# Shorter float64 decoding, sums of magnitudes on ScalarE in place of maxima on VectorE, and another order of the first tiles of the last layer's input product

## The chip, the core and the metric

The kernel runs on one core of one Trainium2 chip. The metric is the device time of one execution in microseconds (us). TensorE multiplies matrices into PSUM, VectorE (DVE in the rows) and ScalarE (ACT) work on tiles in SBUF and PSUM, GpSimd (POOL) on tiles in SBUF, and SyncE (SP) issues nearly all the DMAs. Each engine runs its own instructions strictly in the order of the program, and an instruction that waits holds back all that stand behind it on that engine.

## The reference

The inputs are an attention with mixed heads (batch 4, 12 heads, 448 positions, 64 channels) and two feed-forward blocks over 1792 = 4 x 448 tokens of 768 channels. The change touches only the blocks:

```python
def _moe_ref(x, w1, w2, w3, w_out):
    a = x @ w1
    b = x @ w2
    h = a * b @ w3
    return (h @ w_out).astype(np.float32)

def _moe2_ref(x, w_in, w_out):
    h = x @ w_in
    r = np.maximum(h, 0.0)
    g = r * r
    return (g @ w_out).astype(np.float32)
```

`w1`, `w2` are 768 x 1024, `w3` 1024 x 1024, `w_out` of the first block 1024 x 768, `w_in` of the second 768 x 2048 and its `w_out` 2048 x 768. All eight weight arrays of the two blocks arrive as float64, whose two 32-bit words the kernel turns into float32 itself.

## The kernel before, in words

**Stages.** After the attention (to about 425 us of the span) come the hidden products of the first block (`hidden_tile`, eight columns `fc` of 128 features, four groups of 448 tokens each), then M = w3 x w_out (`m_tile`, so that the two last products of the block become one), then the product of the hidden features with M (here "the x2 stage": four token groups `i`, six tiles `c` each), then the input product of the second block with ReLU and square (`layer_in`, `in_tile`), and the output product in halves of tokens (`multiply`).

**Precision.** Each operand of a product is split into a high and a low half, and three matmuls per pair of tiles add high x high, high x low and low x high. Before a split the tile is scaled by a power of two from the largest magnitude in it (`pow2`). Where the largest value over all 128 partitions is wanted, one number per partition is stored to DRAM and read back broadcast to all partitions: `crossing`, a DMA `across<-...` and then a DMA `ac<-across`, both issued on POOL; then VectorE takes the maximum (`acr<-ac`, line 863).

**Decoding.** `decode` takes a raw chunk of 128 x 768 doubles (`raw`, 768 KB, two buffers, loaded by SP at line 747): ScalarE takes the magnitude of the high word as float32 (`zt`, line 798), VectorE shifts the low word (line 799), clamps `zt` (line 803), joins the two (line 806); ScalarE takes the magnitude of the result in place and adds it up per partition (line 810), and VectorE puts the sign back from `raw` (line 812). `decode_alone` does the same for `w3` without ScalarE at the end. Decoded chunks of `w_in` and the last `w_out` go to DRAM (`kept_in`, `kept_out`) and come back when all chunks of their group of four (`IG`) are summed and the group's scale is known (`cast_in`: `ib<-kept_in` at line 1037, `w<-ib` at lines 1051 and 1052).

**What sets the order.** The program is written by a planner while it is built: `now` advances by fixed costs at every `tick`, `busy` holds a due time for ScalarE, VectorE and POOL, and streams of steps (weights, scales, halves) put their next instruction into the program as soon as the planner's time allows. DMAs of results are put off (`put_later`) and issued by `tick`. `need_in(j)` runs a stream by force when a weight is wanted that has not been written into the program yet.

**Around the first tiles of `layer_in`.** `layer_in((0, 1))` takes four columns `jj` of 128 features, with four token groups `i`: sixteen tiles of 18 matmuls. The scale factor of a tile (`sci`) is the product of the x2 scale `kx` and the weight scale. Twelve tiles (`i` from 0 to 2) come first, then `finish(x2_done[3])`, and the four tiles of `i = 3`, each behind its own `sci` (line 1649). The weights of column pair `q` may be fetched back only once `q <= pair_now[0] + 1`, and `pair_now` is set when `layer_in` of a pair begins. The four buffers of finished weights hold `jj` 0 to 3, and those of `jj` 4 and 5 take the buffers of `jj` 0 and 1.

Of the kernel before, what the change touches and what calls it, by code (L numbers as in the profile page):

```python
# [18 lines left out]
P = 128  # L19
CP = 112  # L20
F64_LEAST = 2.0 ** -15 * 1.125
F64_MOST = float.fromhex("0x1.dffffep+16")
# [13 lines left out]
def talking_heads_attention_moe_moe2(  # L36
# [696 lines left out]
    def load_w(i):  # L733
        kind, j = chunks[i]
        if kind == "wl":
            t = wo_tiles(j)[1]
# [23 lines left out]
    def decode_alone(raw, n):  # L760

        lo, hi = (raw.rearrange("p (f two) -> p f two", two=2)[:, :, w] for w in (0, 1))
        x = pools["w"].tile([P, DM], F32, tag="xa", name="xa", bufs=3)[:, :n]
        zt = pools["w"].tile([P, DM], F32, tag="zt", name="zt", bufs=1)[:, :n]
        xi, zi = x.bitcast(I32), zt.bitcast(I32)
        r = n / DM
        return x, [
            (ACT, 0.9 * r, lambda: nc.scalar.activation(zt, hi.bitcast(F32), AF.Abs)),
            (DVE, 0.55 * r, lambda: nc.vector.tensor_scalar(
                xi, lo, 29, 0x40000000, op0=ALU.logical_shift_right, op1=ALU.bitwise_or  # L770
            )),
            (DVE, 0.95 * r, lambda: nc.vector.scalar_tensor_tensor(
                xi, hi, -(2 ** 31), xi, op0=ALU.bitwise_and, op1=ALU.bitwise_or
            )),
            after(ACT),
            (DVE, 0.55 * r, lambda: nc.vector.tensor_scalar(
                zt, zt, F64_LEAST, F64_MOST, op0=ALU.max, op1=ALU.min
            )),
            (DVE, 0.55 * r, lambda: nc.vector.tensor_scalar(
                zi, zi, 4, 1, op0=ALU.logical_shift_left, op1=ALU.logical_shift_right  # L780
            )),
            (DVE, 0.95 * r, lambda: nc.vector.tensor_tensor(xi, zi, xi, op=ALU.bitwise_xor)),
            after(DVE),
        ]

    def decode(raw, n, total=None, x=None, zt=None):
# [10 lines left out]
        return x, [  # L797
            (ACT, 0.9 * r, lambda: nc.scalar.activation(zt, z, AF.Abs)),
            (DVE, 1.0 * r, lambda: nc.vector.tensor_scalar(
                xi, lo, 29, 0x40000000, op0=ALU.logical_shift_right, op1=ALU.bitwise_or  # L800
            )),
            (REST, HAND, None),
            (DVE, 0.6 * r, lambda: nc.vector.tensor_scalar(
                zt, zt, F64_LEAST, F64_MOST, op0=ALU.max, op1=ALU.min
            )),
            (DVE, 1.0 * r, lambda: nc.vector.scalar_tensor_tensor(  # L806
                xi, zt.bitcast(I32), 3, xi, op0=ALU.logical_shift_left, op1=ALU.bitwise_xor
            )),
            (REST, HAND, None),
            (ACT, 1.0 * r, lambda: nc.scalar.activation(x, x, AF.Abs, accum_out=total)),  # L810
            (REST, HAND, None),
            (DVE, 1.0 * r, lambda: nc.vector.scalar_tensor_tensor(
                xi, hi, -(2 ** 31), xi, op0=ALU.bitwise_and, op1=ALU.bitwise_or
            )),
        ]

# [155 lines left out]
    def one_steps(i):  # L972
# [26 lines left out]
        x, ops = (decode_alone if kind == "w3" else decode)(t, n)  # L999
        yield from read_raw(i, x, ops)  # L1000
        if kind == "w3":
            hh, ll = (
                pools["w"].tile([P, 4 * P], F32R, tag="wv"[z], name="w3", bufs=WB) for z in range(2)
            )
        elif j >= NFC // 2:
            yield POOL, 0, lambda: nc.sync.dma_start(kept[j], x)
            return
        else:
            hh, ll = wo_tiles(j)
# [169 lines left out]
    def largest(out, x):  # L1179
# [8 lines left out]
        (c0, c0 + 3, c0 + 4, c0 + 5, c1, c1 + 3, c1 + 4, c1 + 5),  # L1188
        (1, 1, 1, 1, 1, 1, 1, 1),
# [11 lines left out]
    def hidden_tile(ws, sc, hm, i, z, th, pt):  # L1201
        product(pt, [(two(ws[z][0]), cols_of(c), x) for c, x in enumerate(x_parts())], toks(i))
        if z == 0:
            nc.scalar.activation(th, pt[:, :S], AF.Copy, scale=sc[:, 0, i : i + 1])
            tick(1.13, 0.6)
        else:
# [3 lines left out]
            largest(hm[:, i : i + 1], th)  # L1210
            tick(1.13, 0, 1.2)
# [105 lines left out]

    def stage():
        return mlp.tile([P, S], F32, tag="st", name="st", bufs=16)
# [29 lines left out]
    hs = []  # L1349
    for fc in range(NFC):  # L1350
# [13 lines left out]
        for i in range(len(ths), B):  # L1364
            th = stage()
            for z in range(2):
                hidden_tile(ws, sc, hm, i, z, th, mm())
            ths.append(th)
        nc.vector.tensor_reduce(hm[:, B : B + 1], hm[:, :B], axis=AX.X, op=ALU.max)
        up, lo = pow2(hm[:, B : B + 1], 14, "hs")  # L1370
        nc.vector.tensor_copy(rows[:, 0, fc : fc + 1], lo)
        t = mp.tile([P, 2, NT], F16, tag="h", name="h", bufs=NFC)
        streams.append(Stream(halves_steps(
            [((t[:, 0, toks(i)], t[:, 1, toks(i)]), ths[i], up) for i in range(B)]
        )))
# [12 lines left out]
    def keep_m(f, acc, os_):  # L1388
# [132 lines left out]
    def x2_steps(i, ts, xm):  # L1521
# [5 lines left out]

        yield from crossing(xm[:, NDC:], 1, box, DVE)
# [6 lines left out]
    for i in range(B):  # L1535
# [3 lines left out]
        for c in range(NDC):  # L1539
# [4 lines left out]
            largest(xm[:, c : c + 1], pt[:, :S])  # L1544
            ts.append(t)
            if c < NDC - 1:
                tick(1.13, 0.6, 0.6)
        for o in range(2):
            a = slice(3 * o, 3 * o + 3)
            nc.vector.tensor_scalar(xm[:, a], xm[:, a], mlo[o], None, op0=ALU.mult)  # L1550
        nc.vector.tensor_reduce(xm[:, NDC:], xm[:, :NDC], axis=AX.X, op=ALU.max)
        x2_done.append(Stream(x2_steps(i, ts, xm)))
        streams.insert(0, x2_done[-1])
        tick(1.13, 0.6, 0.8)
# [78 lines left out]
    def layer_in(ps, gm):  # L1633
# [7 lines left out]
        n = B if ps[0] else B - 1  # L1641
# [305 lines left out]
```

## Time and profile before

| | |
|---|---|
| median of 3 runs | 1259.68 us (1258.32 to 1266.53) |
| the profiled execution | 1259.91 us, its span 1258.2 us |
| PE busy | 1233.0 us, 98% of the span |
| DVE, ACT, POOL busy | 926.9, 758.1, 527.1 us |
| granted TensorE clock, mean | 0.995 of full speed |

The profile counts an engine as busy while an instruction of it runs, and puts idle time down to what ended it. Line numbers (L1162) are those of the kernel before; names such as `mm<-x,w` read "tile written <- tiles read". In the columns of a stretch the granted clock is 1.00 at 2.4 GHz and 0.50 at 1.2 GHz.

### The profile page before, as it was taken

The page shows a single profiled execution, that of the slowest core. Times are in us where ns is not written, and L with a number is a line of the kernel's source. Part 1 is how long each engine was busy: PE and PEld are TensorE (multiplying, and loading weights), DVE is VectorE, ACT ScalarE, POOL GpSimd, SP SyncE. Part 2 cuts the span into 40 slices and gives each one's busy share as a digit, 9 for nine tenths or more (in the row PEclk, how much of TensorE's full clock was granted, in tenths as well). Part 3 has the DMA queues.
Part 4 walks back from the last instruction along what each step waited for, and adds up shares of the span by engine and source line. Part 5 has one row for each costly group of instructions (what it writes and reads, how often), then busy time and mean ns, then how long its engine had stood idle before and what let it go on. Part 6 is the DMA issues. An engine that isn't in the chain of part 4 may idle for free. (4 is left out here: it accounts for less than half of the span.)

```text
span 1258.2 us, 26105 instructions
## 1 busy us (share of the span) xinstructions
PE 1233.0 (98%) x10022; PEld 759.0 (60%) x10022; DVE 926.9 (74%) x1744; ACT 758.1 (60%) x1502; POOL 527.1 (42%) x537
## 2 busy tenths in 40 slices
PE   8999999999999999999999999999799999999998
PEld 4666666766776655555569955555355555665565
DVE  6888898798889858886849675765433664899673
ACT  6888888888888634543424353546664786665330
POOL 4897898889778401010003200000000414787340
PEclk9999999999999999999999999999899999999999
DMA  6456456555656734354313237567779876566562
GB/s 189 127 158 171 123 146 160 150 139 143 168 145 170 223 61 129 80 110 122 125 69 133 101 110 171 117 119 210 232 199 214 257 239 187 160 202 198 167 181 89
DMA packets 134562, 194.80 MB, mean 155 GB/s; under 512 B 33668, under 2 KB 111108, under 8 KB 134436
## 3 DMA queue, kind: packets, MB, share of 16 engines
q1 hardware_dynamic: 129972, 189.00, 53.9%
q0 software_dynamic: 1328, 1.72, 1.4%
q10 hardware_dynamic: 3136, 2.40, 0.7%
q8 instruction: 79, 1.29, 0.4%
q14 instruction: 47, 0.39, 0.1%
HBM read 109.88 MB, written 44.66 MB: 123 GB/s over the span
## 5 line engine op out<-in xcount | busy, mean ns | idle before, releaser
L1162 PE MATMUL mm<-x,w 128*128 128x448 f16 x2196 | 417.5, 353 | 8.2 <-ACT w L1051 8.1
L1162 PEld LDWEIGHTS <-w 128*128 128x128 f16 x2304 | 225.1, 98 | 219.5 <-ACT w L1051 8.5
L1779 PE MATMUL mm<-ow,ao 128*128 128x384 f16 x1176 | 191.7, 326 | 2.6 <-DVE st L1795 2.5
L285 PE MATMUL p<-Bt,wpre_k 120*120 120x448 f32 x360 | 159.3, 560 | 4.0 <-DMA Bt<-S 3.4
L1779 PEld LDWEIGHTS <-ao 128*128 128x128 f16 x1176 | 115.1, 98 | 79.2 <-issue 3.3
L381 PEld LDWEIGHTS <-EH 120*112 120x112 f16 (+1 forms) x1440 | 124.5, 130 | 44.0 <-issue 36.9
L403 DVE TENSOR_TENSOR ATl<-o,ATh 112x480 f16<-112x480 f32 x180 | 116.2, 645 | 24.2 <-ACT ATh L397 23.5
L354 POOL TENSOR_SCALAR EH<-E,st 120x448 f16<-120x448 f32 (+1 forms) x152 | 114.5, 761 | 44.3 <-DVE st L337 32.4
L307 ACT ACTIVATE E<-p,st 120x448 f32<-120x448 f32 x180 | 116.0, 644 | 21.4 <-DVE st L299 13.5
L397 ACT CAST ATh<-o 112x480 f16<-112x480 f32 x180 | 101.0, 561 | 42.6 <-PE o L381 37.8
L381 PE MATMUL o<-wph,EH 120*112 120x120 f16 x720 | 124.0, 219 | 0.8 <-DVE ATl L403 0.5
L381 PE MATMUL o<-wph,EL 120*112 120x120 f16 x720 | 122.0, 216 | 0.0
L381 PE MATMUL o<-wpl,EH 120*112 120x120 f16 x720 | 122.0, 216 | 0.0
L366 POOL TENSOR_TENSOR EL<-F,EH 120x448 f16<-120x448 f32 (+1 forms) x90 | 104.6, 1162 | 33.1 <-issue 20.1
L299 DVE TENSOR_REDUCE st<-p 120x1 f32<-120x448 f32 x180 | 110.2, 613 | 0.9 <-PE p L285 0.6
L1162 PE MATMUL mm<-h,M 128*128 128x448 f16 x576 | 109.8, 353 | 0.7 <-ACT M L1340 0.5
L810 ACT ACTIVATE xa<-xa 128x768 f32<-128x768 f32 x54 | 45.4, 841 | 88.6 <-DVE xa L806 80.1
L381 PEld LDWEIGHTS <-EL 120*112 120x112 f16 x720 | 93.6, 130 | 0.0
L368 DVE SCALAR_TENSOR_TENSOR EL<-E,st,EH 120x448 f16<-120x448 f32 (+1 forms) x90 | 82.7, 919 | 10.7 <-POOL EH L354 10.3
L1162 PEld LDWEIGHTS <-M 128*128 128x128 f16 x576 | 55.9, 98 | 53.9 <-DVE M L1336 2.1
L249 ACT COPY S<-s 110x896 f32<-110x896 f32 (+1 forms) x88 | 80.4, 913 | 9.7 <-PE s L242 8.9
L285 PEld LDWEIGHTS p<-Bt,wpre_k 120*120 120x120 f32 x360 | 57.1, 182 | 47.9 <-issue 17.9
(241 smaller groups left out, 2163.8 us busy)
## 6 DMA issues: line engine op xcount, KB each, us to landing
Bt<-S SPq DMA_DIRECT2D x176, 210.0 KB
raw<-in_moe_w_out_dram SPq DMA_DIRECT2D x24, 768.0 KB
g<-st SPq DMA_DIRECT2D x64, 224.0 KB
gt<-g SPq DMA_DIRECT2D x56, 256.0 KB
raw<-in_moe_w_in_dram SPq DMA_DIRECT2D x16, 768.0 KB
raw<-in_moe_w_dram SPq DMA_DIRECT2D x14, 768.0 KB
raw<-in_moe_w_dram SPq DMA_DIRECT2D x16, 512.0 KB
kept_in<-xa SPq DMA_DIRECT2D x16, 384.0 KB
```

The source lines that it names most:

```text
L249: nc.scalar.copy(Stile[s][:R, 2 * p : 2 * p + 2, :], Ps.pop((s, p))[:R, :, :S])
L285: nc.tensor.matmul(pt[: n * H, :S], wpre_k.rearrange("p t g -> p (t g)")[: n * H, : n * H], Bt.pop(u)[: n * H], start=True, stop=True,)
L299: nc.vector.tensor_reduce(nsum[u][:n, 0, j : j + 1], Pp[u][:n, :S], axis=AX.X, op=ALU.max, negate=True)
L307: nc.scalar.activation(e[:n], Pp.pop(u)[:n, :S].rearrange("p (a b) -> p a b", a=EG), AF.Exp, bias=t[:n, 0, j : j + 1], scale=1.0, accum_ou ...
L354: nc.gpsimd.tensor_scalar(seven(EH[u][:n]), Ex[u][:n], inverse(u), 1.0, op0=ALU.mult, op1=ALU.mult)
L366: nc.gpsimd.tensor_tensor(a, f, b, op=ALU.subtract)
L368: nc.vector.scalar_tensor_tensor(a, e, inverse(u), b, op0=ALU.mult, op1=ALU.subtract)
L381: nc.tensor.matmul(pt[:CP, c * n : (c + 1) * n], a[:n, c * CP : (c + 1) * CP], w[:n, :n], start=(i == 0), stop=(i == 2),)
L397: nc.scalar.copy(ATs[s][0][:, :, :, m * NR : m * NR + nr], src)
L403: nc.vector.tensor_tensor(ATs[s][1][:, :, :, a], src, ATs[s][0][:, :, :, a], op=ALU.subtract)
L1162: nc.tensor.matmul(pt[:, :S], w[a][:, cs], x[z][:, sl], start=(c == 0 and i == 0), stop=(c == len(parts) - 1 and i == 2),)
L1779: nc.tensor.matmul(pt[:, :OH], y[:, a, q * P : (q + 1) * P], ow[g, q][:, w, kb], start=(start and q == 0 and m == 0), stop=(q == NQ - 1 an ...
```

## The change

Six things change. (1) `decode` scales the high word by 2^-112 in the ScalarE pass, and the clamp on VectorE goes; the sign is joined before the last step, so that `raw` is read for the last time one VectorE step earlier and ahead of ScalarE's sum, which now writes into `zt` and is left out where no sum is wanted; `decode_alone` goes, and `w3` uses `decode`. (2) The maxima over the hidden tiles (except the first three token groups of column 0), over the x2 tiles and over M (except its last row tile) become sums of magnitudes on ScalarE (`magnitudes`), written to a tile `junk` that nobody reads. (3) The scale of a hidden column becomes a stream (`h_steps`). (4) The maximum over the six columns of an x2 group moves from the main program into its stream (`x2_steps`). (5) Stores to `kept` are put off. (6) In the first `layer_in` ten tiles come first, then six: (0,3), (1,3), (2,2), (2,3), (3,2), (3,3), and `pair_now` becomes 1 after the second of them.

```diff
-F64_LEAST = 2.0 ** -15 * 1.125
-F64_MOST = float.fromhex("0x1.dffffep+16")
+F64_BIAS = 2.0 ** -112
...
         if kind == "wl":
+            flush("kept")
...
-    def decode_alone(raw, n):
...
-            (ACT, 0.9 * r, lambda: nc.scalar.activation(zt, z, AF.Abs)),
-            (DVE, 1.0 * r, lambda: nc.vector.tensor_scalar(
-                xi, lo, 29, 0x40000000, op0=ALU.logical_shift_right, op1=ALU.bitwise_or
+            (ACT, 0.9 * r, lambda: nc.scalar.activation(zt, z, AF.Abs, scale=F64_BIAS)),
+            (DVE, 0.6 * r, lambda: nc.vector.tensor_scalar(
+                xi, lo, 29, 0, op0=ALU.logical_shift_right, op1=ALU.bitwise_or
             )),
-            (REST, HAND, None),
-            (DVE, 0.6 * r, lambda: nc.vector.tensor_scalar(
-                zt, zt, F64_LEAST, F64_MOST, op0=ALU.max, op1=ALU.min
+            (DVE, 1.0 * r, lambda: nc.vector.scalar_tensor_tensor(
+                xi, hi, -(2 ** 31), xi, op0=ALU.bitwise_and, op1=ALU.bitwise_or
             )),
+            (REST, 0.3, None),
             (DVE, 1.0 * r, lambda: nc.vector.scalar_tensor_tensor(
                 xi, zt.bitcast(I32), 3, xi, op0=ALU.logical_shift_left, op1=ALU.bitwise_xor
             )),
-            (REST, HAND, None),
-            (ACT, 1.0 * r, lambda: nc.scalar.activation(x, x, AF.Abs, accum_out=total)),
-            (REST, HAND, None),
-            (DVE, 1.0 * r, lambda: nc.vector.scalar_tensor_tensor(
-                xi, hi, -(2 ** 31), xi, op0=ALU.bitwise_and, op1=ALU.bitwise_or
-            )),
         ]
+        if total is not None:
+            ops += [
+                after(DVE),
+                (ACT, 1.0 * r, lambda: nc.scalar.activation(zt, x, AF.Abs, accum_out=total)),
+            ]
...
+                magnitudes(*n_mags.pop())
+                tick(1.13, 1.4)
...
+                n_mags.append((hm[:, i : i + 1], th))
+                tick(1.13, 0, 0.65)
...
+    def magnitudes(out, x):
+        nc.scalar.activation(junk[:, : x.shape[-1]], x, AF.Abs, accum_out=out)
...
+    def h_steps(fc, hm, t, ths):
...
+        for a in last:
+            yield ACT, 0.8, lambda: magnitudes(*a)
+        yield after(ACT)
+        yield DVE, 1.4, scale
...
-                yield DVE, 0.45, lambda: largest(mx[:, f, o : o + 1], M32[f][o])
+                yield ACT, 0.75, lambda: magnitudes(mx[:, f, o : o + 1], M32[f][o])
...
+        yield after(ACT)
+        yield DVE, 0.3, lambda: nc.vector.tensor_reduce(
+            xm[:, NDC:], xm[:, :NDC], axis=AX.X, op=ALU.max
+        )
         yield from crossing(xm[:, NDC:], 1, box, DVE)
...
-            largest(xm[:, c : c + 1], pt[:, :S])
+            magnitudes(xm[:, c : c + 1], t)
...
-        n = B if ps[0] else B - 1
+        late = [] if ps[0] else [(jj, B - 1) for jj in (0, 1)] + [
+            (jj, i) for jj in (2, 3) for i in (B - 2, B - 1)
+        ]
+        early = [(jj, i) for jj in sc for i in range(B) if (jj, i) not in late]
+        n = B - 1 if late else B
...
-        for jj, i in [(jj, i) for jj in sc for i in range(n)]:
+        for jj, i in early:
             in_tile(gm, jj, i, *sc[jj])
-        if n < B:
+        if late:
             finish(x2_done[n])
             for jj in sc:
                 nc.vector.tensor_scalar(sc[jj][1][:, n:], kx[:, n:], need_in(jj)[1], None, op0=ALU.mult)
-                in_tile(gm, jj, n, *sc[jj])
+        for jj, i in late:
+            in_tile(gm, jj, i, *sc[jj])
+            if (jj, i) == (1, B - 1):
+                pair_now[0] = 1
```

**SyncE, the fetch of the weights of `jj` 4 to 7.** `ib<-kept_in` are these fetches, `g<-st` stores of finished tiles, `raw` loads of chunks. Before:

```order
L1127 DMA g_12890<-st 128x448 x3
L1127 DMA kept_out_350<-xa 128x768
L1127 DMA g_12890<-st 128x448 x6
L1037 DMA ib<-kept_in_332 128x768
L1037 DMA ib<-kept_in_333 128x768
L1037 DMA ib<-kept_in_334 128x768
L1037 DMA ib<-kept_in_335 128x768
```

And now:

```order
L1102 DMA g_12805<-st 128x448
L1102 DMA kept_out_350<-xa 128x768
L1102 DMA g_12805<-st 128x448 x4
L1012 DMA ib<-kept_in_332 128x768
L1012 DMA ib<-kept_in_333 128x768
L1102 DMA g_12805<-st 128x448 x4
L1012 DMA ib<-kept_in_334 128x768
L1012 DMA ib<-kept_in_335 128x768
```

The fetch for `jj` 4 and 5 stood behind the stores of fifteen tiles of `layer_in`, and stands behind those of ten.

**VectorE, around the scale of x2 group 3 (`xs`, from line 863 on, in the change line 837).** `im` is the top of a group of four weight chunks, `xa<-...` are steps of a decoding. Before, after five decodings without the last step of the fifth:

```order
L806 SCALAR_TENSOR_TENSOR xa<-zt,xa 128x768
L1026 TENSOR_REDUCE im<-isum 128x1
L863 TENSOR_REDUCE acr<-ac 128x1
L109 TENSOR_SCALAR xs<-acr 128x1
L110 TENSOR_SCALAR xs<-xs 128x1
```

And now, after five whole decodings:

```order
L780 SCALAR_TENSOR_TENSOR xa<-zt,xa 128x768
L1001 TENSOR_REDUCE im<-isum 128x1
L773 TENSOR_SCALAR xa<-raw 128x768
L776 SCALAR_TENSOR_TENSOR xa<-raw,xa 128x768
L837 TENSOR_REDUCE acr<-ac 128x1
L108 TENSOR_SCALAR xs<-acr 128x1
```

Two steps of a sixth decoding, which read the sixth chunk, stand ahead of the scale.

**VectorE, around the tile scales of `i = 3` (`sci`, 128x1).** `is` is the scale of a group of weight chunks, here of the third group. Before:

```order
L863 TENSOR_REDUCE acr<-ac 128x1
L109 TENSOR_SCALAR is<-acr 128x1
L110 TENSOR_SCALAR is<-is 128x1
L113 TENSOR_SCALAR is<-is 128x1
L114 RECIPROCAL is<-is 128x1
L1649 TENSOR_SCALAR sci<-kx,is 128x1 x4
L1052 SCALAR_TENSOR_TENSOR w<-ib,is,w 128x768 x2
```

And now:

```order
L1656 TENSOR_SCALAR sci<-kx,is 128x1 x4
L837 TENSOR_REDUCE acr<-ac 128x1
L108 TENSOR_SCALAR is<-acr 128x1
L109 TENSOR_SCALAR is<-is 128x1
L112 TENSOR_SCALAR is<-is 128x1
L113 RECIPROCAL is<-is 128x1
L1027 SCALAR_TENSOR_TENSOR w<-ib,is,w 128x768 x2
```

The four `sci` stand ahead of the scale of the third weight group. TensorE's rows are the same ones in the same sequence, but for the tiles that `layer_in` takes in another order.

## Rows read from the trace of the kernel before

**Rows 1.** The page: busy us, share of the span and instructions of each engine.

```profile
PE 1233.0 (98%) x10022; PEld 759.0 (60%) x10022; DVE 926.9 (74%) x1744; ACT 758.1 (60%) x1502; POOL 527.1 (42%) x537
```

**Rows 2.** Waits of PE: tile and line, what ended it, us in total, times, longest.

```profile
PE mm L1779 <- DVE st L1795: 2.5, 2, 1.8
...
PE mm L1409 <- POOL w L1013: 0.7, 2, 0.5
...
PE mm L1409 <- ACT w L1010: 0.4, 1, 0.4
```

**Rows 3.** Timeline around the gap: start, us, engine, line, instruction, [idle before <- releaser].

```profile
854.83 20.40 PE L1162 MATMUL mm<-x,w 128*128 128x448 f16 x107
...
882.82 6.46 SPq L1127 DMA_DIRECT2D g<-st  x6
...
885.00 0.29 DVE L863 TENSOR_REDUCE acr<-ac 128x1 f32<-128x128 f32 x1 [6.82 <-DMA ac<-across]
...
886.26 0.63 ACT L1656 ACTIVATE st<-mm,sci 128x448 f32<-128x448 f32 x1 [2.95 <-DVE sci L1649]
...
889.33 2.34 SPq L1037 DMA_DIRECT2D ib<-kept_in  x4
...
894.04 1.96 ACT L1051 ACTIVATE w<-ib,is 128x768 f16<-128x768 f32 x2 [2.79 <-DMA ib<-kept_in]
...
895.03 17.23 PE L1162 MATMUL mm<-x,w 128*128 128x448 f16 x81 [8.07 <-ACT w L1051]
```

**Rows 4.** Stretches of PE: from:to, length, busy us (instructions), granted clock, DMA share, GB/s.

```profile
892.00:893.00 1.00, 0.00 (x0) 0.50 1.21 344
...
898.00:899.00 1.00, 1.00 (x6) 0.87 0.00 0
```

**Rows 5.** Timeline of the first tiles of `layer_in` and of the decodings beside them.

```profile
828.09 0.92 ACT L798 ACTIVATE zt<-raw 128x768 f32<-128x768 f32 x1 [6.74 <-DMA raw<-in_moe_w_out_dram]
...
832.32 48.02 PE L1162 MATMUL mm<-x,w 128*128 128x448 f16 x253
...
839.09 1.13 ACT L1543 ACTIVATE st<-mm,ms 128x448 f32<-128x448 f32 x2
...
842.04 0.55 DVE L799 TENSOR_SCALAR xa<-raw 128x768 int32<-128x768 int32 x1
...
846.04 0.33 SPq L747 DMA_DIRECT2D raw<-in_moe_w_in_dram  x1
...
851.15 0.54 POOL L848 DMA_DIRECT2D ac<-across  x1 [7.97 <-DMA across<-xm]
855.43 0.92 ACT L798 ACTIVATE zt<-raw 128x768 f32<-128x768 f32 x1 [6.51 <-DMA raw<-in_moe_w_in_dram]
...
859.93 0.33 SPq L747 DMA_DIRECT2D raw<-in_moe_w_out_dram  x1
...
865.48 0.93 ACT L798 ACTIVATE zt<-raw 128x768 f32<-128x768 f32 x1 [2.68 <-DMA raw<-in_moe_w_out_dram]
...
867.98 0.28 DVE L863 TENSOR_REDUCE acr<-ac 128x1 f32<-128x128 f32 x1
...
869.05 3.46 ACT L1340 ACTIVATE x<-st,xs 128x448 f16<-128x448 f32 x6
```

**Rows 6.** Groups of instructions by shape: count, busy us, mean ns, idle before and its releasers.

```profile
L812 DVE SCALAR_TENSOR_TENSOR xa<-raw,xa 128x768 int32<-128x768 int32 x54 | 52.4, 970 | 31.6 <-ACT xa L810 31.6
...
L803 DVE TENSOR_SCALAR zt<-zt 128x768 f32<-128x768 f32 x55 | 31.3, 569 | 14.2 <-ACT zt L798 14.2
...
L1180 DVE TENSOR_REDUCE hm<-st 128x1 f32<-128x448 f32 x29 | 18.0, 620 | 1.0
```

**Rows 7.** The same view: ScalarE's square of a tile and the read of its sum.

```profile
L1657 ACT ACTIVATE st<-st 128x448 f32<-128x448 f32 x64 | 36.9, 577 | 2.0
...
L1657 ACT ACTIVATION_READ_ACCUMULATOR st<-st 128x1 f32 x64 | 11.9, 186 | 0.0
```

**Rows 8.** Stretch 722 to 832 us, the x2 stage: PE, PEld, DVE, ACT, POOL busy, clock, DMA.

```profile
722.00:832.00 110.00, 109.53 (x578) 56.26 (x579) 71.37 (x141) 49.97 (x88) 6.20 (x10) 1.00 0.59 135
```

More of the change, by code (lines that the diff above doesn't have):

```diff
@@ L998, in one_steps @@
             return
-        x, ops = (decode_alone if kind == "w3" else decode)(t, n)
+        x, ops = decode(t, n)
         yield from read_raw(i, x, ops)
+        yield after(DVE)
         if kind == "w3":
@@ L1209, in hidden_tile @@
             )
-            largest(hm[:, i : i + 1], th)
-            tick(1.13, 0, 1.2)
+            if n_mags is None:
+                largest(hm[:, i : i + 1], th)
+                tick(1.13, 0, 1.2)
+            else:
+                n_mags.append((hm[:, i : i + 1], th))
+                tick(1.13, 0, 0.65)
     def first_tile(n):
@@ L1316, in mm @@
         return ps_m.tile([P, 512], F32, tag="mm", name="mm")
+    junk = mlp.tile([P, S], F32, tag="junk", name="junk", bufs=1)
+    def magnitudes(out, x):
+        nc.scalar.activation(junk[:, : x.shape[-1]], x, AF.Abs, accum_out=out)
     def stage():
@@ L1348, in talking_heads_attention_moe_moe2, with scale @@
     kx = sm.tile([P, B], F32, tag="kx", name="kx", bufs=1)
-    hs = []
+    hs, mags = [], []
+    def h_steps(fc, hm, t, ths):
+        box = {}
+        def scale():
+            nc.vector.tensor_reduce(hm[:, B : B + 1], hm[:, :B], axis=AX.X, op=ALU.max)
+            box["up"], lo = pow2(hm[:, B : B + 1], 14, "hs")
+            nc.vector.tensor_copy(rows[:, 0, fc : fc + 1], lo)
+        last = list(mags)
+        mags.clear()
+        yield after(DVE)
+        for a in last:
+            yield ACT, 0.8, lambda: magnitudes(*a)
+        yield after(ACT)
+        yield DVE, 1.4, scale
+        yield from halves_steps(
+            [((t[:, 0, toks(i)], t[:, 1, toks(i)]), ths[i], box["up"]) for i in range(B)]
+        )
     for fc in range(NFC):
@@ L1366, in talking_heads_attention_moe_moe2 @@
             for z in range(2):
-                hidden_tile(ws, sc, hm, i, z, th, mm())
+                hidden_tile(ws, sc, hm, i, z, th, mm(), mags)
             ths.append(th)
-        nc.vector.tensor_reduce(hm[:, B : B + 1], hm[:, :B], axis=AX.X, op=ALU.max)
-        up, lo = pow2(hm[:, B : B + 1], 14, "hs")
-        nc.vector.tensor_copy(rows[:, 0, fc : fc + 1], lo)
         t = mp.tile([P, 2, NT], F16, tag="h", name="h", bufs=NFC)
-        streams.append(Stream(halves_steps(
-            [((t[:, 0, toks(i)], t[:, 1, toks(i)]), ths[i], up) for i in range(B)]
-        )))
+        streams.append(Stream(h_steps(fc, hm, t, ths)))
         hs.append(two(t))
@@ L1543, in talking_heads_attention_moe_moe2 @@
             nc.scalar.activation(t, pt[:, :S], AF.Copy, scale=mlo[c // 3])
-            largest(xm[:, c : c + 1], pt[:, :S])
+            magnitudes(xm[:, c : c + 1], t)
             ts.append(t)
             if c < NDC - 1:
[L1547 to L1551, printed above, removed]
+                tick(1.13, 1.35)
         x2_done.append(Stream(x2_steps(i, ts, xm)))
         streams.insert(0, x2_done[-1])
-        tick(1.13, 0.6, 0.8)
+        tick(1.13, 1.35)
     mid.close()
```

39 lines of the change are left out of this document (10 added, 29 removed).

## The prediction, made before the kernel was run

> **What bounds the kernel now.** I read the busy times first: TensorE is busy for 1233.0 of 1258.2 us [rows 1]. About 25 us can be won at all, whatever the change does for the other engines; the question is which of TensorE's idle times it touches. The waits of TensorE and the timeline say where these are: one gap of 8.07 us [rows 3], 1.1 us on the weights `w3` and 1.8 us, the longest of two, in the output product [rows 2]. The rest lies at the start and in the attention, where almost nothing changes.
>
> The gap is read backwards [rows 3]. TensorE waits for weights `jj` = 4 that ScalarE splits at 894.04. ScalarE waits for their fetch, which SyncE issued at 889.33 although nothing but its place in the queue held it: it stands behind six stores of tiles, and they wait for ScalarE's tiles. ScalarE waits 2.95 us for a tile scale on VectorE, and VectorE stands idle 6.82 us for the `ac<-across` of a weight group that is wanted much later. So the gap comes from the order of instructions in three queues. After it TensorE runs at 0.50 of its clock until the stretch from 898 [rows 4]: 81 matmuls take 17.23 us, where at the rate of the 107 before the gap (20.40 us) they would take 15.44. That is 1.79 us, including the wait for the low half of the first weight.
>
> **The change part by part.**
>
> *Decoding.* VectorE loses a clamp, 0.57 us, from each of the 54 chunks (the 55 calls of the row hold one for a shared buffer) and 29 maxima of 0.62 us [rows 6], then 24 over x2 and 14 over M of similar length. It is not the bound, so this counts only where it feeds TensorE. The place is `w3`: per chunk two short steps less, so high and low halves come earlier than the 0.4 and 0.7 us by which TensorE waited [rows 2]. Bounds: nothing, and 1.1 us; I take 1.1, since the two steps are most of a microsecond and three waits share it. If this cover were missing, the old waits are what returns.
>
> *Sums on ScalarE.* 67 of them, 0.58 us and 0.19 us for the read of the sum by the nearest row, the square of the same shape [rows 7]: 51 us on ScalarE, against which eight sums of chunks go. It was busy for 758.1 us of the span [rows 1]. In the x2 stage, the densest of the stages concerned, it would go from 49.97 us of 110 to 68 [rows 8]. What hides them is TensorE's own work: it is busy for 109.53 of these 110 us. A maximum takes 0.62 us, a sum 0.76, so the move would cost 67 x 0.14 = 9 us on a chain, and costs nothing as long as the tiles wait in PSUM. The Trainium skill, in "ScalarE: Activation LUTs" (rules for kernel authors), says that maxima and other simple arithmetic belong on VectorE rather than on ScalarE. The single instruction agrees with it, 0.62 against 0.76 us; by that rule the sum would be 9 us worse, by the rows of the stage it is not.
>
> *Order of the first tiles.* A tile takes (886.96 - 832.32) / 16 = 3.415 us, with 886.96 the start of the gap, 895.03 - 8.07 [rows 3, 5]. The fetch for `jj` 4 now stands behind the stores of ten tiles and no longer fifteen, and the scales of the tiles stand ahead of the `ac<-across` that held VectorE. So the gap of 8.07 us and its 1.79 us of slow clock go, if the fetch is in time (below).
>
> *What is late next.* x2 group 3 is now wanted after ten tiles, at 832.32 + 34.15 = 866.47, and no longer after twelve, at 873.3. Before, its halves began at 869.05 [rows 5]: 4 us ahead of the old need, but 2.6 us behind the new one. Its scale was not waiting for its crossing: `acr` at 867.98 shows no idle time before it [rows 5]. It stood behind five decodings, each behind its raw chunk. Now two steps of a sixth stand there too. Against that, a raw buffer comes free earlier: before, the load for the third chunk went out at 846.04, 4.0 us after the first step of the first chunk at 842.04; now it can go out after two VectorE steps, 0.55 + 0.97 = 1.5 us. A load takes 9.4 us (846.04 to 855.43) or 5.55 (859.93 to 865.48) [rows 5]. With these: chunk 1 frees its buffer at 843.6, chunk 2 at 846.4 (behind the sum of chunk 1 and its own first pass on ScalarE); chunk 3 arrives at 853.0, chunk 4 at 855.8, and ScalarE takes chunk 4 up to 857.4 behind the sum of chunk 3. Chunk 6 then arrives between 863.0 and 866.8. Two steps (1.5), `acr` to the first half (869.05 - 867.98 = 1.07) and a high and a low half (1.2, from 3.46 us for six) put the first columns at 866.8 to 870.6. TensorE waits 0.3 to 4.1 us at tile (0,3); I take 2.2, the middle, since both load times occur in this stretch. Below it the bound is nothing.
>
> *The fetch.* ScalarE must finish ten tiles before the tenth store. From the scale of group 3, at 865.6 to 869.4, it has six halves (3.46), five tiles of 0.63 + 0.58 + 0.19 = 1.4 and one sum (1.0) to do: 877.0 to 880.9. A fetch takes 4.7 us (889.33 to 894.04) [rows 3], or 9.4 like a raw chunk: it lands between 881.7 and 890.3. Tile 17 starts at 886.96 and the new wait, 887.3 to 891.1, and its first high half needs 0.98 us on ScalarE ahead of that. So it is in time, or late by about 1 us with the longest fetch. I take 0.
>
> *The sum*: -8.07 - 1.79 - 1.1 + 2.2 = -8.8 us, against the profiled execution's 1259.91: 1251.1. This execution stands 0.23 above the median of the runs, 1259.68, so the forecast is **1251** (1250.9). Ends: without the new wait and with the 1.8 us of the output product gone as well, 1247; with 4.1 us of waiting, 1 us for the fetch and no gain at `w3`, 1256.
>
> **The rivals.**
>
> *No new wait at all* (0.25). If loads of chunks take 5.5 us or less in this stretch, because fewer of them collide with the stores, group 3 is ready in time, and the time is 1259.68 - 10.96 = 1249. For it speaks the one load of 5.55 us, against it the two of 9.4 [rows 5]. The Trainium skill, in "DMA: Bandwidth & Descriptors" (anatomy of one DMA), gives a copy about 2.0 us plus its bytes at 436 GB/s, an estimate of 3.8 us for 768 KB. By that rule the sixth chunk would come at 861 and this rival would be the result; the trace disagrees, with 9.4 us.
>
> *The gap moves* (0.13). The fetch still stands behind ten stores in SyncE's queue, and these behind ScalarE, which also waits for raw chunks (6.51 us at 855.43 [rows 5]). One more such wait among tiles 6 to 10 moves the fetch from 877.0 to 880.9 to 883.5 to 887.4 and its landing to 888 to 897: TensorE waits 1 to 6 us more and may fall to the half clock again (1.8). That gives 1253 to 1259, about 1256.
>
> *ScalarE falls behind, and the kernel is slower* (0.10). The place is the x2 stage: ScalarE alone empties the tiles, and waits for raw chunks in its queue (6.74 us at 828.09). Before, it took the last two x2 tiles at 839.09, ending 7.9 us after TensorE was done with them at 832.32 [rows 5]. If none of its waits takes up the added sums, 24 x 0.76 = 18 us, the last x2 sum comes at 858. The crossing then decides: `ac<-across` waited 7.97 us for its first leg [rows 5], the second let VectorE idle for 6.82 us [rows 3], with their issue about 16. With 2.3 us of scale and halves the first columns come at 876.5, 10 us late, and 1.8 us of slow clock follow: 1259.68 - 10.96 + 11.8 = 1260.5. From about 16 us of lateness on, this eats the whole gain; each further 3.4 us is a tile more. Against it: ScalarE stood idle for 60 of the 110 us [rows 8], so most of the sums fit there.
>
> *My forecast* has 0.52.
>
> **How the numbers follow.** The likeliest case gives 1251. The range is 1247.5 to 1257.5: down to the case without a new wait less about one microsecond for the smaller waits, up past the forecast's own end of 1256 into most of the case where the gap moves. Outside lie the slower case and the tails, under 0.2. A difference of under 1%, 12.6 us, is about what this measurement can't tell from none. All the idle time that the change can reach, 8.07 + 1.79 + 1.1 + 1.8 = 12.8 us, is no more than that: faster by over 1% gets 0.05. Slower by over 1%, above 1272, needs the last rival with three more tiles lost: 0.04. The rest, 0.91, is within 1%, nearly all of it on the faster side.
>
> **What would show it.** The gap of 8.07 us before the weights of `jj` 4 should be gone and the clock stay at 1.00 there; SyncE's `ib<-kept_in` should go out near 879, and the four `sci` stand ahead of an idle VectorE. A wait of TensorE of 0 to 4 us should appear about 34 us after the first tile of `layer_in`, released by the halves of x2 group 3. The waits on `w3` should shrink below 0.3 us. VectorE's busy time should fall by some 90 us and ScalarE's rise by 45, without any change of the time from either. The forecast is wrong if the wait at group 3 is above 5 us, if TensorE still waits for `ib`, or if waits appear among the hidden or x2 tiles, where there are none now.

## The result, and the profile after

The changed kernel takes **1248.26 us** (median of 6 runs, 1247.43 to 1249.23) beside 1261.05 us for the kernel before (6 runs, 1258.32 to 1266.53) on the same chip: a ratio of 0.9896, 95% interval 0.9875 to 0.9916. The profiled execution took 1248.55 us, its span is 1246.8 us. The time is that of the rival without a new wait, 1249, and lies in the range; the forecast of 1251 was one term too high.

The page gives the busy time of each engine, to be read against [rows 1]:

```profile
PE 1230.0 (99%) x10022; PEld 757.8 (61%) x10022; DVE 845.8 (68%) x1581; ACT 793.6 (64%) x1628; POOL 523.9 (42%) x537
```

VectorE lost 81 us and ScalarE gained 36, both less than the 90 and 45 expected. Of TensorE's waits (what for, us in total, times, longest), the two on `w3` [rows 2] are gone; the output product still waits:

```profile
PE mm L1789 <- DVE st L1805: 2.4, 2, 1.7
```

The groups by shape (count, busy us, mean ns, idle before) show what replaced the clamp, the last sign step and the maxima of [rows 6]:

```profile
L780 DVE SCALAR_TENSOR_TENSOR xa<-zt,xa 128x768 int32<-128x768 int32 x54 | 52.9, 979 | 37.5 <-ACT zt L772 34.2
L776 DVE SCALAR_TENSOR_TENSOR xa<-raw,xa 128x768 int32<-128x768 int32 x54 | 52.4, 971 | 1.9
...
L1304 ACT ACTIVATE junk<-st 128x448 f32<-128x448 f32 x53 | 30.4, 573 | 14.8 <-DVE st L1186 14.1
...
L1304 ACT ACTIVATION_READ_ACCUMULATOR junk<-st 128x1 f32 x67 | 12.7, 190 | 0.0
```

The sign step on VectorE costs the same 0.97 us as in [rows 6], but its idle time ahead of it fell from 31.6 to 1.9 us, since it no longer stands behind ScalarE. The idle time has not gone: it has moved to the last step (L780), which stands idle for 37.5 us, 34.2 of them for ScalarE's first pass. What is gained is that `raw` has been read by then. The two rows of a sum, 0.573 and 0.190 us, add up to the 0.76 us estimated from [rows 7], but they overlap in time: one sum starts at 825.29, its read at 825.78 and ScalarE's next instruction at 825.87. What a sum costs is read below, from the kernel with the maxima put back. In the x2 stage (722 to 831 us: PE, PEld, DVE, ACT, POOL busy, clock, DMA) TensorE stays covered, as in [rows 8]:

```profile
722.00:831.00 109.00, 108.90 (x577) 56.32 (x577) 58.31 (x116) 69.58 (x140) 5.46 (x10) 1.00 0.65 148
```

The timeline of the stretch that [rows 3] and [rows 5] show of before (start, us, engine, line, instruction, idle before):

```profile
831.27 73.94 PE L1137 MATMUL mm<-x,w 128*128 128x448 f16 x390
...
833.09 0.56 DVE L773 TENSOR_SCALAR xa<-raw 128x768 int32<-128x768 int32 x1
...
834.73 0.33 SPq L747 DMA_DIRECT2D raw<-in_moe_w_in_dram  x1
...
838.00 0.33 SPq L747 DMA_DIRECT2D raw<-in_moe_w_in_dram  x1
...
846.81 0.93 ACT L772 ACTIVATE zt<-raw 128x768 f32<-128x768 f32 x1 [6.37 <-DMA raw<-in_moe_w_in_dram]
...
858.97 0.93 ACT L772 ACTIVATE zt<-raw 128x768 f32<-128x768 f32 x1 [1.15 <-DMA raw<-in_moe_w_out_dram]
...
861.53 2.91 ACT L1328 ACTIVATE x<-st,xs 128x448 f16<-128x448 f32 x5 [1.63 <-DVE kx L1529]
...
866.85 0.57 DVE L1656 TENSOR_SCALAR sci<-kx,is 128x1 f32<-128x1 f32 x4
...
872.32 1.28 SPq L1012 DMA_DIRECT2D ib<-kept_in  x2
...
875.54 0.29 DVE L837 TENSOR_REDUCE acr<-ac 128x1 f32<-128x128 f32 x1 [8.12 <-DMA ac<-across]
...
880.38 1.74 ACT L1026 ACTIVATE w<-ib,is 128x768 f16<-128x768 f32 x2
```

The first row is the result: 390 matmuls in one piece, where before 107 were followed by 8.07 us of nothing. The fetch of the weights of `jj` 4 goes out at 872.32 and they are split from 880.38 on; their tile comes at 831.27 + 16 x 3.41 = 885.9. The 8.12 us that VectorE idles for the crossing of a weight group are still there, now behind the four `sci` and so with nobody waiting. The clock (stretch, busy, granted clock), which was 0.50 at 892 to 893 in [rows 4]:

```profile
890.00:895.00 5.00, 5.00 (x28) 1.00 0.93 295
```

### The profile page after: what moved, and what is told of

It reads as the page before. It is cut to its first block, busy times and chain, and to the rows that moved or that the text cites. A ratio compares the mean times of both kernels' runs of the same rounds, so it can differ in the third digit from the quotient of the medians.

```text
span 1246.8 us, 26161 instructions
## 1 busy us (share of the span) xinstructions
PE 1230.0 (99%) x10022; PEld 757.8 (61%) x10022; DVE 845.8 (68%) x1581; ACT 793.6 (64%) x1628; POOL 523.9 (42%) x537
## 4 chain that ended last, share of the span: by engine, by line
PE 89%; DVE 5%; DMA 3%; ACT 2%; issue 0%; SPq 0%; ACTq 0%; POOL 0%; DVEq 0%
PE mm L1137 42%; PE mm L1789 15%; PE p L284 9%; PE o L380 7%; PE mm L1412 5%; PE s L241 5%; PE a L494 4%; DMA Bt<-S 2%; PE p L1137 2%; DVE ATl L402 1%; DVE st L298 1%; DVE EL L367 1%; DMA x<-x_d 1%; ACT E L306 1%; DMA vraw<-in_v_dram 0%
## 5 line engine op out<-in xcount | busy, mean ns | idle before, releaser
L380 PEld LDWEIGHTS <-EH 120*112 120x112 f16 (+1 forms) x1440 | 124.4, 130 | 44.7 <-issue 37.5
L780 DVE SCALAR_TENSOR_TENSOR xa<-zt,xa 128x768 int32<-128x768 int32 (+1 forms) x70 | 69.4, 991 | 51.0 <-ACT zt L772 47.4
```

What stands on the lines that cost most here:

```text
L380: nc.tensor.matmul(pt[:CP, c * n : (c + 1) * n], a[:n, c * CP : (c + 1) * CP], w[:n, :n], start=(i == 0), stop=(i == 2),)
```

## The experiments

Theory A, the prediction's: the fetch's place in SyncE's queue and the scales' place in VectorE's make the gap, and the new order removes it, while the earlier need for x2 group 3 brings a wait of its own. Rivals: the gain comes from the lighter work of VectorE, or from other parts of the reordering. The first four kernels shared 13 runs of the kernel before (median 1262.49 us), the next four 10 runs (1260.58) and the last two 11 runs (1261.94).

**The old order of tiles in the changed kernel.**

```diff
...
-        for jj, i in early:
+        for jj, i in [(jj, i) for jj in sc for i in range(n)]:
             in_tile(gm, jj, i, *sc[jj])
...
                 nc.vector.tensor_scalar(sc[jj][1][:, n:], kx[:, n:], need_in(jj)[1], None, op0=ALU.mult)
-        for jj, i in late:
-            in_tile(gm, jj, i, *sc[jj])
-            if (jj, i) == (1, B - 1):
-                pair_now[0] = 1
+                in_tile(gm, jj, n, *sc[jj])
```

> The changed kernel with the tiles of the first layer_in in the old order (twelve, then four) and no early release of the weight pair; decoding and sums as changed. Theory A (the gap is made by the order in three queues, the faster decoding only shortens it): the fetch ib<-kept_in stands behind 14 stores, goes out near 880.6 us and lands 4.7 to 7.4 us later, TensorE wants jj 4 at 885.9: a gap of 0.4 to 4 us returns, 1249 to 1252.5 us. Rival B (decoding alone removed the gap, the order is not needed): no gap, 1248.3. Rival C (the order alone removed it): the whole gap with its slow clock is back, about 1258.

Measured: 1253.54 us (1252.52 to 1254.48), ratio 0.9932 (0.9908 to 0.9957). Its timeline around the gap:

```profile
831.52 54.64 PE L1137 MATMUL mm<-x,w 128*128 128x448 f16 x288
...
888.41 0.55 PE L1137 MATMUL mm<-x,w 128*128 128x448 f16 x2 [2.25 <-ACT w L1026]
889.47 15.72 PE L1137 MATMUL mm<-x,w 128*128 128x448 f16 x74 [0.50 <-DVE w L1027]
...
881.12 1.88 SPq L1012 DMA_DIRECT2D ib<-kept_in  x4
```

and a stretch of it (length, busy, granted clock):

```profile
889.00:893.00 4.00, 3.53 (x11) 0.57 0.01 1
```

The gap is back behind sixteen tiles, but as 2.25 + 0.50 us: decoding, sums and the other reorderings had already brought the fetch from 889.33 [rows 3] to 881.12. At the 0.190 us a matmul of the changed kernel's piece (73.94 / 390), 74 of them take 14.0 us, so the slow clock costs 1.7. Together 4.5 us, and the ratios differ by 0.0036 x 1261 = 4.5 us. Theory A holds by its gap; the time is 1 us above its range, which had no term for the clock. Rivals B and C are refuted.

**The new order of tiles without the release of the next weights.**

```diff
         for jj, i in late:
             in_tile(gm, jj, i, *sc[jj])
-            if (jj, i) == (1, B - 1):
-                pair_now[0] = 1
```

> The changed kernel with the new order of tiles, but the pair of weights not released after the second late tile. Theory A (the release is what moves the fetch ahead of four stores): the fetch stands behind 14 stores instead of 10, goes out near 880.6, and a gap of 0.4 to 4 us is back before jj 4; 1249 to 1252.5. Rival (the order of the tiles and of the scales is what counts, the release nothing): 1248.3, no gap.

Measured: 1254.27 us (1251.95 to 1254.5), ratio 0.9934 (0.9909 to 0.996). Its timeline:

```profile
889.07 0.55 PE L1137 MATMUL mm<-x,w 128*128 128x448 f16 x2 [2.25 <-ACT w L1026]
...
881.78 1.87 SPq L1012 DMA_DIRECT2D ib<-kept_in  x4
```

The same gap and, within the intervals, the same time as with the old order, again above the range for want of the clock. The scales of the tiles are early here: the four `sci` go out at 867.73 us, ahead of the crossing that holds VectorE until 876.74, where in the old order they follow at 877.66. By itself that is worth nothing. What the order part gives in the changed kernel comes from the two lines that let the fetch out behind ten stores.

**The new order alone, in the kernel before.** The tile order and the release of the change, and nothing else of it.

```diff
...
-        for jj, i in [(jj, i) for jj in sc for i in range(n)]:
+        for jj, i in early:
...
+        for jj, i in late:
+            in_tile(gm, jj, i, *sc[jj])
+            if (jj, i) == (1, B - 1):
+                pair_now[0] = 1
```

> The kernel before with nothing but the new order of the first layer_in (ten tiles, then six, pair released after the second). Theory A: the fetch comes in time and the gap at jj 4 is gone (-9.9 us), but x2 group 3, whose halves began at 869.05, is wanted at 866.5: TensorE waits about 3.8 us there; about 1255 us. Rival B (the gap goes by decoding): the gap stays, 1258 or more. Rival C (order alone is enough): no new wait, 1250 to 1251.

Measured: 1258.54 us (1256.43 to 1260.63), ratio 0.9973 (0.9961 to 0.9985). Its timeline at group 3:

```profile
833.17 34.21 PE L1162 MATMUL mm<-x,w 128*128 128x448 f16 x180
871.27 0.53 PE L1162 MATMUL mm<-x,w 128*128 128x448 f16 x1 [3.89 <-ACT x L1340]
871.99 23.12 PE L1162 MATMUL mm<-x,w 128*128 128x448 f16 x109 [0.19 <-DVE x L1336]
...
870.55 3.46 ACT L1340 ACTIVATE x<-st,xs 128x448 f16<-128x448 f32 x6
```

and the stretch behind the wait:

```profile
872.00:876.00 4.00, 4.00 (x11) 0.50 0.07 24
```

Here is the wait that the prediction put into the sum, after exactly ten tiles, at 3.89 us; and a stretch at 0.50 of the clock behind it, which no expectation had: 23.12 us against 109 x 0.190 = 20.7, so 2.4 us. The old gap at `jj` 4 is 0.50 us, but only because TensorE itself is about 7 us late there: the fetch goes out at 884.36, where the changed kernel has it at 872.32. So the order by itself trades one gap for another, at a gain of 3.4 us (0.0027 x 1262), and the time is 3.5 us above Theory A's 1255.

**The old decoding in the changed kernel.** `decode` and `decode_alone` of before put back (four VectorE passes for a chunk and five for `w3`, instead of three, with ScalarE's sum ahead of the last), with sums and order of the change. The planner's waits inside the chain and its table of early decoding steps (`STEPS`) go back with them.

```diff
-            (ACT, 0.9 * r, lambda: nc.scalar.activation(zt, z, AF.Abs, scale=F64_BIAS)),
+            (ACT, 0.9 * r, lambda: nc.scalar.activation(zt, z, AF.Abs)),
...
+                zt, zt, F64_LEAST, F64_MOST, op0=ALU.max, op1=ALU.min
...
+            (ACT, 1.0 * r, lambda: nc.scalar.activation(x, x, AF.Abs, accum_out=total)),
+            (REST, HAND, None),
             (DVE, 1.0 * r, lambda: nc.vector.scalar_tensor_tensor(
-                xi, zt.bitcast(I32), 3, xi, op0=ALU.logical_shift_left, op1=ALU.bitwise_xor
+                xi, hi, -(2 ** 31), xi, op0=ALU.bitwise_and, op1=ALU.bitwise_or
             )),
...
-        (c0, c0 + 3, c0 + 4, c1, c1 + 3, c1 + 4),
-        (1, 1, 1, 1, 1, 1),
+        (c0, c0 + 3, c0 + 4, c0 + 5, c1, c1 + 3, c1 + 4, c1 + 5),
+        (1, 1, 1, 1, 1, 1, 1, 1),
```

> The changed kernel with the decoding of before (clamp, ScalarE in the middle of the chain, raw read last by VectorE's sign step); sums on ScalarE and the new order stay. Theory A (the decoding that frees raw early is what made x2 group 3 early): halves of group 3 begin near 869 again, wanted at 866: a wait of 2 to 5 us there, and the 1.1 us on w3 are back; 1251 to 1254. Rival (the maxima that left VectorE made it early): no wait at group 3, 1248.5 to 1249.5.

Measured: 1252.06 us (1250.91 to 1255.05), ratio 0.9918 (0.9889 to 0.9947). Its timeline at group 3:

```profile
833.17 34.21 PE L1164 MATMUL mm<-x,w 128*128 128x448 f16 x180
868.64 0.35 PE L1164 MATMUL mm<-x,w 128*128 128x448 f16 x1 [1.26 <-ACT x L1355]
...
838.15 0.56 DVE L800 TENSOR_SCALAR xa<-raw 128x768 int32<-128x768 int32 x1
...
867.92 1.23 ACT L1355 ACTIVATE x<-st,xs 128x448 f16<-128x448 f32 x2 [0.88 <-DVE kx L1556]
```

One row of TensorE's waits, and the stretch behind the first piece:

```profile
PE mm L1439 <- POOL w L1015: 0.7, 2, 0.4
```

```profile
870.00:873.00 3.00, 2.16 (x8) 0.70 0.85 55
```

Theory A by its time, half way by its halves: the wait at group 3 is 2.5 us in four pieces (the first is shown; 0.37, 0.48 and 0.36 follow), the granted clock falls even behind these pieces, and one of the two waits on `w3` is back. The profile is that of the slowest of the four executions, 1255.05 us, so the waits of the median one may be shorter.

**The maxima on VectorE again.** The program of the changed kernel, with each of the 67 sums replaced by a maximum on VectorE.

```diff
     def magnitudes(out, x):
-        nc.scalar.activation(junk[:, : x.shape[-1]], x, AF.Abs, accum_out=out)
+        largest(out, x)
```

> The changed kernel in its own order, with the one difference that each of the 70 sums of magnitudes on ScalarE is the dense maximum on VectorE again (569 ns each in [rows 6], about 40 us more VectorE work and about 50 us less ScalarE work). Theory A (the changed order moves the fetch, and the shorter ScalarE chain lets the x2 copies end early): VectorE has slack in every stretch but the end of the attention and the output products, so the time is that of the changed kernel to within 1 us (ratio to the kernel before 0.989 to 0.991), the group-3 wait stays away, and the halves of group 3 start before 865 us. Theory B (VectorE's relief by the sums is what brings the x2 work forward): halves of group 3 late by 2 to 4 us, a wait of TensorE of that size at group 3, 1252 to 1254 us. Aside: the 1.1 us that the changed kernel idles more at the attention's end goes away under either if ScalarE's sums cause it.

Measured: 1250.38 us (1249.08 to 1251.83), ratio 0.9917 (0.99 to 0.9934); the changed kernel beside it 1248.67 us (1248.51 to 1250.56), 0.9906 (0.989 to 0.9923). Its timeline at group 3:

```profile
831.90 36.67 PE L1137 MATMUL mm<-x,w 128*128 128x448 f16 x193
868.97 36.30 PE L1137 MATMUL mm<-x,w 128*128 128x448 f16 x190 [0.40 <-DVE x L1324]
...
864.28 2.91 ACT L1328 ACTIVATE x<-st,xs 128x448 f16<-128x448 f32 x5 [1.64 <-DVE kx L1529]
```

And its page:

```profile
PE 1230.9 (99%) x10022; PEld 758.2 (61%) x10022; DVE 886.6 (71%) x1648; ACT 755.0 (60%) x1494; POOL 523.1 (42%) x537
```

The halves begin 32.4 us behind the first tile of `layer_in`, where the changed kernel beside it has 31.6, and one low half, the last of six, is 0.40 us late. Neither is more than executions of the changed kernel's own program differ by, as the last experiment shows. The medians differ by 1.7 us, more than the 1 us expected, but the intervals overlap: theory A by size, and the exchange of maxima for sums is worth 0 to 2 us. By the pages, 67 sums cost ScalarE 793.6 - 755.0 = 38.6 us, 0.58 each, and 67 maxima cost VectorE 886.6 - 845.8 = 40.8 us, 0.61 each: the two instructions take about the same time. (The 569 ns of the expectation is the clamp's row; a maximum has 620 ns in [rows 6].) The idle time at the end of the attention, which the aside asked about, stays: TensorE is busy 52.7 of 55 us (375 to 430), 52.8 in the changed kernel and 53.9 before. It is 52.6 in the kernel with the new order alone, which is the kernel before up to there, so this differs by execution and not by the change.

**One pass more on VectorE.** Each decoded chunk gets a clamp that changes no value; added work.

```diff
-            (DVE, 1.0 * r, lambda: nc.vector.scalar_tensor_tensor(
+            (DVE, 1.0 * r, lambda: (nc.vector.tensor_scalar(
+                zt, zt, 0.0, 3.0e38, op0=ALU.max, op1=ALU.min
+            ), nc.vector.scalar_tensor_tensor(
...
```

> The changed kernel with one VectorE pass more on every decoded 128x768 tile (a clamp that changes no value), 70 passes, at the place in the chain where VectorE joins the two halves; the planned order is the same. Theory A (order): the pass lengthens the VectorE chain by about 0.6 us a chunk, which its slack takes; 1248 to 1250 us, at most the 1.1 us of waits of the third product back. Theory B (a shorter decoding chain is itself the gain): most of the 11 us is lost again, 1255 us or more.

Measured: 1250.49 us (1249.4 to 1251.61), ratio 0.9918 (0.99 to 0.9935). Its timeline at group 3:

```profile
870.15 1.13 PE L1139 MATMUL mm<-x,w 128*128 128x448 f16 x5 [0.53 <-DVE x L1326]
...
864.86 2.91 ACT L1330 ACTIVATE x<-st,xs 128x448 f16<-128x448 f32 x5 [1.61 <-DVE kx L1531]
```

Some 40 us of VectorE work cost 1.8 us by the medians and 1.5 by the ratios, whose intervals overlap: 0 to 2 us, and 0.53 us is seen at group 3. Theory A, with a time 0.5 us beyond its range; Theory B is refuted. The waits on `w3` do not come back with one pass more; with the two more of the old decoding, one does.

**Eight tiles early instead of ten.**

```diff
-            (jj, i) for jj in (2, 3) for i in (B - 2, B - 1)
+            (jj, i) for jj in (2, 3) for i in (B - 3, B - 2, B - 1)
```

> The changed kernel with eight instead of ten input tiles of the first pairs put early (tile 1 of pairs 2 and 3 goes to the late list). TensorE then reaches the first tile that needs group 3 at about 831.3 + 8 x 3.41 = 858.6 us instead of 865.4, and the halves of group 3 begin at 861.5 and end at about 864. Theory A (ten early tiles are what covers the chain of group 3): a wait of 3 to 5 us at group 3, and after it a stretch at the half clock as behind the waits of 2.25 and 3.9 us in the two runs before, 1 to 3 us; 1252 to 1256 us. Theory B (the number of early tiles is of no matter, the chain follows the products): no wait, the time of the changed kernel.

Measured: 1256.24 us (1255.06 to 1257.44), ratio 0.9963 (0.9951 to 0.9974). Its timeline at group 3, and the stretch behind the wait:

```profile
830.63 27.40 PE L1137 MATMUL mm<-x,w 128*128 128x448 f16 x144
862.58 0.53 PE L1137 MATMUL mm<-x,w 128*128 128x448 f16 x1 [4.54 <-ACT x L1328]
863.30 42.00 PE L1137 MATMUL mm<-x,w 128*128 128x448 f16 x207 [0.19 <-DVE x L1324]
...
861.86 2.91 ACT L1328 ACTIVATE x<-st,xs 128x448 f16<-128x448 f32 x5 [1.64 <-DVE xs L113]
```

```profile
864.00:868.00 4.00, 4.00 (x12) 0.50 0.95 50
```

Theory A, at the upper end of its numbers (the time 0.2 us above it): the halves come at their time, TensorE is there two tiles earlier and waits 4.54 + 0.19 us; 207 matmuls take 42.00 us instead of 39.2, so 2.8 for the clock. The sum, 7.5, is the difference to the changed kernel (1256.24 - 1248.67 = 7.6).

**The changed kernel beside them**, twice.

> The changed kernel itself, on the same chip as the three variants, so that they are compared with it there: ratio 0.988 to 0.992 to the kernel before, no wait at group 3 and no gap at the fetch of pair 4.

> The changed kernel again beside it, for the comparison: ratio 0.988 to 0.992 to the kernel before, a wait of 1.7 to 1.8 us for the output tile near 1154 us.

1248.67 us (ratio as above) and 1248.11 us (1247.57 to 1248.96, 0.9894, 0.9876 to 0.9913). Neither profile has a wait at group 3, and the second has the wait for the output tile at 1154.09 us, 1.79 us long, as expected. The first:

```profile
831.41 73.94 PE L1137 MATMUL mm<-x,w 128*128 128x448 f16 x390
...
863.00 2.91 ACT L1328 ACTIVATE x<-st,xs 128x448 f16<-128x448 f32 x5 [1.64 <-DVE kx L1529]
```

and the second:

```profile
830.29 218.08 PE L1137 MATMUL mm<-x,w 128*128 128x448 f16 x1152
...
859.95 2.91 ACT L1328 ACTIVATE x<-st,xs 128x448 f16<-128x448 f32 x5 [1.63 <-DVE kx L1529]
```

**An attempt at the last wait**, that of the output product.

```diff
         elif p == NP2 - 1:
-            streams.append(mixed_out(1))
+            streams.insert(0, mixed_out(1))
```

> The changed kernel with one word changed: the stream that mixes the second group of output weights is put at the head of the list of background work instead of its end, so that part of its VectorE passes leaves the stretch from 1100 to 1160 us, where VectorE is busy 57.9 of 60 us and TensorE waits 1.74 us for an output tile. If that queue is what TensorE waits for there: 1 to 1.7 us less than the changed kernel on the same chip, and no wait above 1 us in that stretch. Rival: the planned order only exchanges which output tile is late, and the time stays within 0.5 us.

Measured: 1254.22 us (1253.78 to 1256.32), ratio 0.9945 (0.993 to 0.9961): slower than the changed kernel by 6.1 us. Two waits in its timeline:

```profile
1132.88 25.20 PE L1789 MATMUL mm<-ow,ao 128*128 128x384 f16 x154 [1.66 <-DVE ao L1732]
1160.70 19.54 PE L1789 MATMUL mm<-ow,ao 128*128 128x384 f16 x110 [2.62 <-DVE st L1805]
```

The clock behind each of the two waits:

```profile
1133.00:1137.00 4.00, 4.00 (x26) 1.00 0.92 282
...
1161.00:1165.00 4.00, 4.00 (x18) 0.65 0.00 0
```

Both expectations missed. The weights, mixed earlier, now stand ahead of the token halves (`ao`) in VectorE's queue, which become late (2.7 us in three waits), and the output tile is later than before (2.62 instead of 1.79 us) with the lower clock behind it. Waits and clock account for about 4.8 of the 5.0 us that the output product takes longer. The profiled execution, the slowest of the six, had lost another 3 us ahead of it, which the edit doesn't touch: up to there this is the program of the changed kernel. Its rows at group 3 therefore show how much executions of that one program differ:

```profile
832.55 36.67 PE L1137 MATMUL mm<-x,w 128*128 128x448 f16 x193
869.74 181.77 PE L1137 MATMUL mm<-x,w 128*128 128x448 f16 x959 [0.52 <-DVE x L1324]
...
865.05 2.90 ACT L1328 ACTIVATE x<-st,xs 128x448 f16<-128x448 f32 x5 [1.63 <-DVE kx L1529]
```

The halves begin 32.5 us behind the first tile, and the last low half is 0.52 us late, as with the maxima on VectorE and with the extra pass.

## Why the prediction came out as it did

**The gap goes.** Right, with its clock: -8.07 and -1.79, one piece of 390 matmuls at 1.00. The reason held in part. The kernel with the old order shows that decoding, sums and the other reorderings alone take the gap from 8.07 to 2.75 us, because the chain in front of ScalarE's tiles runs ahead; the release of the fetch behind ten stores takes the rest, 4.5 us with the clock. I had put all of it down to the order. The other half of my reason, the place of the scales, gives nothing without the release.

**`w3`.** Right at 1.1 us: both waits are gone, 89.35 us busy from 640 to 730 where it was 88.22.

**Sums on ScalarE at no cost in the x2 stage.** Right: TensorE is busy 108.90 of 109 us. The price of 0.76 us was too high, since it added two rows that overlap; put back, the maxima show 0.58 us for a sum and 0.61 for a maximum, so that the 9 us "on a chain" would not have been there either. The Trainium skill, in "ScalarE: Activation LUTs" (rules for kernel authors), wants maxima on VectorE. With them back there the kernel is no faster, 1250.38 against 1248.67 us.

**The new wait, +2.2.** This step failed: in all three profiles of the changed kernel it measured nothing. "Chunk 1 frees its buffer at 843.6" carried the start of the first decoding, 842.04, over from the kernel before. It began at 833.09. Taken from the start of `layer_in` (832.32 before, 831.27 after), the first chunk moved from 9.7 to 1.8 us, because ScalarE was done with the x2 copies and the halves of group 2 that much earlier. From there the order of steps was as I had it: the third load out 1.6 us after the first step (estimate 1.5), the fourth 4.9 us after it (4.4). The loads themselves were longer, not shorter: 12.1 us (834.73 to 846.81) for the third chunk and 7.0 for the sixth, which went out at 851.94. From its first step to the first half the chain took 28.4 us (833.09 to 861.53), where I had 23.5 to 27.4. Begun at 842.04, it would have made TensorE wait for more than the 4.1 us of my upper bound. So two errors of opposite sign met, and the rival's result came about without its reason: that no wait came was luck as far as my numbers go. The Trainium skill, in "DMA: Bandwidth & Descriptors" (anatomy of one DMA), gives the formula behind the prediction's 3.8 us for copies that GpSimd issues; these loads are issued by SyncE, and at 5.8 to 12.3 us not one of the four was that short.

The kernels above give, from the start of `layer_in`, the first VectorE step of the first decoding and the first half of group 3. Ten tiles last 34.2 us, and the first matmul follows the start of the half by 0.7 (867.92 to 868.64 with the old decoding), so it should start by 33.5:

```
kernel                             first step    first half    wait at group 3
before (need after twelve tiles)   9.7           36.7          none
new order alone                    10.5          37.4          3.9 + 0.2
old decoding                       5.0           34.8          2.5 in four pieces
maxima on VectorE                  2.2           32.4          0.4
extra VectorE pass                 3.2           31.9          0.5
changed kernel, three profiles     1.6 to 1.8    29.7 to 31.6  none
its program, in the last attempt   3.3           32.5          0.5
```

From the first step to the first half all of them take 27 to 30 us. So the lead is gained ahead of the first decoding, while the x2 stage ends. The earlier release of `raw`, on which the prediction counted, did not shorten what follows: 29.8 us with the old decoding, 28.0 to 29.9 in the changed kernel. Read from top to bottom, the sums and the other reorderings are worth 2.6 us of lead with the old decoding (37.4 to 34.8, one profile each), and the shorter decoding on top of them 2.3 to 5.1. What the sums alone add once the decoding is short does not show: maxima and extra pass lie within the 29.7 to 32.5 us of the changed kernel's own program. The margin to 33.5 is 1 to 4 us, and at its lower end the last low half is already half a microsecond late. No run takes back the changes (3) to (5), so their share stays open, and so does which part of the shorter decoding counts. The mechanism of the wait was right: it stands after ten tiles wherever the lead is missing, and after eight with eight tiles.

**The sum.** Without that term it is -8.07 - 1.79 - 1.1 = -10.96, and 1259.91 - 10.96 = 1248.95; the profiled execution took 1248.55. The remaining 0.4 us is a balance of smaller ones that differ by execution: the attention's end idles 1.1 us more, and the granted clock of the first 60 us was 0.97 in the profile before and 1.00 in this one, but also 0.97 in the profile without the release and in that of the last attempt. By the medians of the same measurement the change is worth 12.8 us, 1.8 more than the terms; the runs of the kernel before spread over 8 us there, and no profile shows where those 1.8 lie. That is a gain of 1.04% (0.84 to 1.25), so over 1% was about as likely as not, where the prediction gave it 0.05. The upper end of the prediction, with 4.1 us of waiting, 1 us for the fetch and nothing at `w3`, adds up to 1255 and not to 1256, which leaves the range as it is.

**The other rivals.** The gap did not move: the fetch went out at 872.32, 5 to 9 us ahead of my estimate. ScalarE did not fall behind: it took up the first decoding 1.6 us after TensorE had ended the x2 stage, where before its last x2 copies ended 7.9 us after it.

## What to carry to other kernels

A chain of steps that starts from a time of the old profile must be checked for what the change does ahead of that start: here the same change that made a wait possible had moved its chain by 8 us. A fetch that waits only for its place in a queue is freed by a release a few tiles earlier, but the release pays only when the data that the reordered tiles need comes earlier too; alone, it turned one gap into another. And moving work forward on an engine with no room delays what it overtakes.

## What the runs showed of the hardware

TensorE's granted clock fell behind shorter waits than the 8 us of before. Behind 3.89 and 4.54 us it was at the lower level (0.50, 1.2 GHz) for the 4 us shown. Behind 2.25 us (followed by another 0.50), 2.62 us, and four waits of 1.26 us and less in a row it was 0.57, 0.65 and 0.70 in the stretches shown. That cost 1.5 to 2.8 us more each time. Behind the 1.74 us of the changed kernel's output product (1152 to 1160) and the 1.66 us above, it stayed at 1.00. So in these five cases a stretch of waits of 2.5 to 4.7 us cost some 1.6 times its length. Loads of the same 768 KB took between 5.8 and 12.3 us within 25 us of one execution.
